# Decoding, splitting and storing a kernel's weights in tiles of 1024 columns instead of 512

## The chip, the cores and the metric

The kernel runs on one core of a Trainium2 chip. The core has TensorE (PE, matrix products), VectorE (DVE), ScalarE (ACT) and GpSimd (POOL) for work on tiles, and SyncE (SP), which here issues all DMAs. Each engine takes its instructions in the order of its own queue. The metric is device time in microseconds (us), the median of several runs; the profile is of one execution.

## What is computed

Causal attention with a decay bias, then two feed-forward layer pairs, all in float32. The inputs are q, k and v of 4 batches, 8 heads, 576 tokens and 64 columns, so 2304 tokens of 512 columns pass the layers:

```python
scores = scale * np.matmul(q, k.transpose(0, 1, 3, 2))
cum = np.cumsum(np.maximum(s, 0.0), axis=-1)
bias = -(cum[:, :, :, None] - cum[:, :, None, :])
scores = np.where(causal, -1000000000.0, scores + np.minimum(bias, 0.0))
attn = softmax(scores)                          # divided by (sum + 1e-09)
x = np.matmul(attn, v)                          # 2304 x 512
x = ((x @ w_a) * (x @ w_b)) @ w_out             # 512 -> 1536 -> 512
h = x @ w_in                                    # 512 -> 2048
out = (np.maximum(h, 0.0) + alpha * np.minimum(h, 0.0)) @ w2_out
```

The weights come as 64-bit floats.

## The kernel before

**Tokens and layers.** The 2304 tokens are taken in five blocks, four of 512 and one of 256 (block 4). `ffn` runs the two layer pairs for a block; the attention of the next block is cut into steps that are laid between its matmuls. A weight tile is 128 x 512; there are 68 (`NW`), and each block uses all of them in the same order, 36 in the first layer pair and 32 in the second. PE multiplies in three parts for precision: a weight tile and its input are each split into a high and a low part (`wh`, `wl`; `xh`, `xl`; `gh`, `gl`), and `mm3` adds high x high, high x low and low x high. So a tile costs PE twelve matmuls.

**The first pair** (`into`, `copy_a`, `gate`): in a step, two tiles make a and b in two PSUM banks, ACT copies a (`a_sb`), DVE multiplies it by b (`g`), and g is split into `gh` (ACT) and `gl` (DVE or POOL). One step later a third tile multiplies it into the output. After the last step there are no tiles for a and b, so the last output tile follows right behind the one before it. **The second pair** (`into`, `rectify`): one tile makes h, ACT, DVE or POOL, and DVE make `m` and `g` from it, g is split, and two steps later another tile multiplies it.

**Weights in block 0.** A raw tile of 64-bit values is loaded (`first`, buffers `raw`, 6), decoded into 32-bit floats by `decode` (one operation on ACT or POOL, then a shift and two combining operations on DVE, lines 970 and 271; buffers `w32`, 4, named `w` in the profile's rows), split into `wh` and `wl` (`parts`, `split`; buffers of `wsp`, 6), and the decoded tile is stored to DRAM (`store`, tensor `w_d`). A `w32` buffer is free again when it has been split and its store has landed (`keep`). **From block 1 on** (`again`, `load_pair`) two decoded tiles come in one load from `w_d` into a raw buffer and are only split. The split of a tile waits for a `wsp` buffer, which PE gives back with the last matmul of a tile (`run.give(of_w)`). `prefetch` starts the loads up to ten tiles (`AHEAD`) ahead of the one that PE takes.

**Other users of the buffers.** From batch 2 on (`STACK`), `stack` splits keys and queries into two `w32` buffers for each head.

**Order.** The code is written out in a fixed order by a planner (`Order`): chains of operations are Python generators, and each `yield` names the engines that may do the next operation with a time in ns. The planner keeps a clock for each engine, takes the operation that could start first, and lets the cheaper engine do it; `slack` (`SL_LOAD`, `SL_PARTS`) puts weight work behind other work of the same time. `Slots` count buffers: a chain that yields one waits until another gives it back. PE's order is that of the loops. A long operation thus changes where the planner puts all others. `sub` goes to POOL or DVE, `copy` to ACT or DVE; those marked `port` are planned as excluding POOL.

## Time and profile before

| | us |
|---|---|
| median of 3 runs (lowest, highest) | 1017.45 (1015.12, 1019.9) |
| profiled execution | 1020.0 |
| its span, first to last instruction | 1018.2 |
| PE busy | 994.2 |
| DVE busy | 730.7 |
| ACT busy | 562.3 |
| POOL busy | 238.4 |

The busy times are sums over the span, in which a record of a pipelined matmul overlaps the next one's. The page further gives slices of the span, the DMA queues, the chain of work that ended last and the costliest groups of instructions; the trace behind it answers for stretches of time, for single lines and tiles, and for who waited for whom. PE's idle time before an instruction is put down to the work that ended the wait.

### The profile page before, as it was taken

What the parts mean: (1) busy time and instruction counts of PE and PEld (TensorE: products, weight loads), DVE (VectorE), ACT (ScalarE), POOL (GpSimd) and SP (SyncE); (2) the same over time, 40 slices, a digit from 0 to 9 for tenths busy, and PEclk for the clock granted to TensorE, in tenths of its full rate; (3) what the DMA queues carried; (4) which work ended last, traced back from release to release, by engine and by line L of the source; (5) the groups of instructions that cost most, each with busy time, mean ns of one, the idle gap of its engine ahead of it and who ended that gap; (6) DMA issues with size and microseconds to landing.
All of it is one profiled execution on the core that took longest, in us unless ns stands there. A gap on an engine that the chain in (4) does not pass through costs nothing.

```text
span 1018.2 us, 16187 instructions
## 1 busy us (share of the span) xinstructions
PE 994.2 (98%) x5385; PEld 813.5 (80%) x5385; DVE 730.7 (72%) x1702; ACT 562.3 (55%) x1166; POOL 238.4 (23%) x300
## 2 busy tenths in 40 slices
PE   6999999999899999999999999999999999999998
PEld 5567777777678888788888888888888888889997
DVE  6998898899887867777468687964454465546685
ACT  5876565676665455655455355654433354446664
POOL 2031111221013233443232123432010022220032
PEclk9999999999999999999999999999999999999999
DMA  7687968466868767657286757464542623417550
GB/s 191 185 263 257 303 222 269 155 234 217 297 229 262 252 182 242 181 171 230 88 264 208 243 191 221 160 188 156 183 141 72 197 69 129 134 48 260 186 182 26
DMA packets 129893, 195.75 MB, mean 192 GB/s; under 512 B 26576, under 2 KB 62416, under 8 KB 129808
## 3 DMA queue, kind: packets, MB, share of 16 engines
q1 hardware_dynamic: 129808, 194.71, 60.6%
q8 instruction: 42, 0.69, 0.3%
q14 instruction: 43, 0.35, 0.1%
HBM read 157.63 MB, written 37.04 MB: 191 GB/s over the span
## 4 chain that ended last, share of the span: by engine, by line
PE 86%; DVE 7%; DMA 5%; ACT 1%; issue 1%; SPq 0%; POOL 0%; ACTq 0%; DVEq 0%; POOLq 0%
PE bank L1060 19%; PE bank L1061 19%; PE bank L1062 19%; PE bank L1169 6%; PE bank L1170 6%; PE bank L1171 6%; DMA w_d<-w 3%; DVE w L271 3%; PE bank L487 2%; DMA kq<-in_kq_a_dram 2%; PE bank L751 2%; PE bank L691 1%; PE bank L513 1%; PE bank L718 1%; PE bank L758 1%
## 5 line engine op out<-in xcount | busy, mean ns | idle before, releaser
L1060 PE MATMUL bank<-xh,wh 128*128 128x512 f32 (+1 forms) x800 | 300.6, 376 | 3.1 <-DVE g L271 2.3
L1062 PE MATMUL bank<-xh,wl 128*128 128x512 f32 (+1 forms) x800 | 295.2, 369 | 1.0 <-DVE wl L277 0.8
L1061 PE MATMUL bank<-xl,wh 128*128 128x512 f32 (+1 forms) x800 | 294.9, 369 | 0.0
L265 ACT ACTIVATE wh<-raw 128x512 fp32r<-128x512 f32 x268 | 167.6, 627 | 99.0 <-PE bank L1061 59.3
L277 DVE TENSOR_TENSOR wl<-raw,wh 128x512 fp32r<-128x512 f32 x188 | 131.4, 700 | 96.5 <-ACT wh L265 89.4
L277 POOL TENSOR_TENSOR wl<-raw,wh 128x512 fp32r<-128x512 f32 x84 | 110.6, 1317 | 340.4 <-ACT wh L265 309.5
L1060 PEld LDWEIGHTS bank<-xh,wh 128*128 128x128 f32 x800 | 150.8, 188 | 34.6 <-issue 5.2
L1062 PEld LDWEIGHTS bank<-xh,wl 128*128 128x128 f32 x800 | 150.8, 188 | 28.2 <-DVE wl L277 2.3
L1061 PEld LDWEIGHTS bank<-xl,wh 128*128 128x128 f32 x800 | 150.9, 189 | 24.3
L265 ACT ACTIVATE gh<-g 128x512 fp32r<-128x512 f32 (+1 forms) x140 | 82.3, 588 | 75.2 <-DVE g L271 73.0
L1169 PE MATMUL bank<-wh,gh 128*128 128x512 f32 x288 | 114.4, 397 | 0.2 <-ACT wh L265 0.2
L1170 PE MATMUL bank<-wl,gh 128*128 128x512 f32 x288 | 112.8, 392 | 1.3 <-DVE wl L277 1.3
L277 DVE TENSOR_TENSOR gl<-g,gh 128x512 fp32r<-128x512 f32 (+1 forms) x125 | 85.5, 684 | 37.6 <-ACT gh L265 36.0
L1171 PE MATMUL bank<-wh,gl 128*128 128x512 f32 x288 | 112.3, 390 | 0.0
L257 ACT ACTIVATE z<-z,mn 128x128 f32<-128x128 f32 (+4 forms) x144 | 83.0, 579 | 41.6 <-DVE mn L271 41.6
L271 DVE SCALAR_TENSOR_TENSOR w<-raw,w 128x512 int32<-128x512 int32 x136 | 92.2, 702 | 0.1
L1060 PE MATMUL bank<-gh,wh 128*128 128x512 f32 (+1 forms) x240 | 90.6, 377 | 1.6 <-ACT gh L265 1.6
L1061 PE MATMUL bank<-gl,wh 128*128 128x512 f32 (+1 forms) x240 | 88.8, 370 | 0.4 <-DVE gl L277 0.4
L1062 PE MATMUL bank<-gh,wl 128*128 128x512 f32 (+1 forms) x240 | 88.5, 369 | 0.0
L257 ACT ACTIVATE m<-bank 128x512 f32<-128x512 f32 (+1 forms) x80 | 44.3, 553 | 69.9 <-PE bank L1062 69.6
L282 DVE TENSOR_SCALAR m<-m,alpha_sb 128x512 f32<-128x512 f32 (+1 forms) x71 | 34.7, 489 | 47.3 <-ACT m L257 46.2
L265 ACT ACTIVATE a_sb<-bank 128x512 f32<-128x512 f32 (+1 forms) x60 | 33.1, 551 | 64.0 <-PE bank L1062 62.0
(96 smaller groups left out, 1422.3 us busy)
## 6 DMA issues: line engine op xcount, KB each, us to landing
raw<-w_d SPq DMA_DIRECT2D x136, 512.0 KB, 4.5
raw<-in_w_dram SPq DMA_DIRECT2D x68, 512.0 KB, 4.8
w_d<-w SPq DMA_DIRECT2D x68, 256.0 KB, 3.5
kq<-in_kq_a_dram SPq DMA_DIRECT2D x16, 512.0 KB, 5.0
zd<-zt SPq DMA_DIRECT2D x32, 192.0 KB, 3.2
pt<-zd SPq DMA_DIRECT2D x32, 192.0 KB, 3.7
kq<-in_kq_b_dram SPq DMA_DIRECT2D x16, 352.0 KB, 7.5
vb<-in_v_dram SPq DMA_DIRECT2D x80, 64.0 KB, 4.0
```

What stands on the lines that cost most here:

```text
L257: nc.scalar.activation(o, i, func, **k)
L265: nc.scalar.activation(o, i, AF.Copy)
L271: f(*args, **k)
L277: (nc.gpsimd if eng == "pool" else nc.vector).tensor_tensor(o, i0, i1, op=ALU.subtract)
L282: (nc.gpsimd if eng == "pool" else nc.vector).tensor_scalar(o, i, s0, s1, op0=ALU.mult, op1=ALU.mult)
L487: nc.tensor.matmul(d, qs[:, r * P:n], k[:, 0:n], start=i == 0, stop=i == 1)
L1060: nc.tensor.matmul(o, wh, ih, start=first, stop=False)
L1061: nc.tensor.matmul(o, wh, il, start=False, stop=False)
L1062: nc.tensor.matmul(o, wl, ih, start=False, stop=last)
L1169: nc.tensor.matmul(acc[t], gh[:, c], wh, start=first, stop=False)
L1170: nc.tensor.matmul(acc[t], gh[:, c], wl, start=False, stop=False)
L1171: nc.tensor.matmul(acc[t], gl[:, c], wh, start=False, stop=last)
```

## The change

Two tiles are now one unit of 128 x 1024 (`W2`; 34 of them, `NP`). In block 0, `first` loads the two raw tiles in two DMAs into one buffer, and `decode`, the split into `wh` and `wl`, and the store each take the whole unit in one instruction. From block 1 on, `load_four` brings four decoded tiles in one DMA of 1 MB; they are split as two units. `take` hands PE one half of a unit at a time, and `leave_w` gives the split buffer back after the second half. All buffers hold as many bytes as before and half as many units: `raw` 3, `w32` 2, `wsp` 3; `AHEAD` is 5 units. `stack` takes one unit for a head's keys and queries. The planner's times follow the size.

```diff
-FROM_WEIGHTS, AHEAD, FROM_LEAD, FROM_STEPS, STEPS = 2, 10, 3, 4, 3
+FROM_WEIGHTS, AHEAD, FROM_LEAD, FROM_STEPS, STEPS = 2, 5, 3, 4, 3
...
-    wsp = ctx.enter_context(tc.tile_pool(name="wsp", bufs=6))
+    wsp = ctx.enter_context(tc.tile_pool(name="wsp", bufs=3))
...
-    W32, RAW, KQ, VB, CB, KL = 4, 6, 3, 4, 3, 2
+    W32, RAW, KQ, VB, CB, KL = 2, 3, 3, 4, 3, 2
...
-        kh = wraw.tile([P, QA], F32R, name="kh", tag="w32", bufs=W32)
-        qs = wraw.tile([P, QA], F32R, name="qs", tag="w32", bufs=W32)
+        hq = wraw.tile([P, 2 * QA], F32R, name="hq", tag="w32", bufs=W32)
+        kh, qs = hq[:, 0:QA], hq[:, QA:2 * QA]
...
+    W2, NP = 2 * WN, NW // 2
...
-        eng = yield {"act": 517, "pool": 590}, SEEN
+        eng = yield {"act": 90 + 0.833 * W2, "pool": 32 + 1.09 * W2}, SEEN
...
-        yield from dve(WN, 0.52, ts, w, w, 3, None, op0=ALU.logical_shift_left,
+        yield from dve(W2, 0.52, ts, w, w, 3, None, op0=ALU.logical_shift_left,
...
-    def load_pair(i):
+    def load_four(i):
         yield of_raw
-        w = wraw.tile([P, 2, WN], F32, name="raw", tag="raw", bufs=RAW)
-        pairs[i, "w"] = w
-        yield from dma(w, w_d[i:i + 2].rearrange("c p n -> p c n"))
+        n = min(4, NW - i)
+        w = wraw.tile([P, 4, WN], F32, name="raw", tag="raw", bufs=RAW)
+        fours[i, "w"] = w
+        yield from dma(w[:, 0:n, :], w_d[i:i + n].rearrange("c p n -> p c n"))
...
         def first():
             yield of_raw
-            r = wraw.tile([P, 2 * WN], I32, name="raw", tag="raw", bufs=RAW)
-            yield from dma(r, w64[i].bitcast(I32))
+            r = wraw.tile([P, 2 * W2], I32, name="raw", tag="raw", bufs=RAW)
+            for j in range(2):
+                yield from dma(r[:, j * W2:(j + 1) * W2], w64[2 * i + j].bitcast(I32))
             yield of_w32
-            w = wraw.tile([P, WN], I32, name="w32", tag="w32", bufs=W32)
+            w = wraw.tile([P, W2], I32, name="w32", tag="w32", bufs=W32)
...
-            h = wsp.tile([P, WN], F32R, name="wh", tag="wh")
-            l = wsp.tile([P, WN], F32R, name="wl", tag="wl")
+            h = wsp.tile([P, W2], F32R, name="wh", tag="wh")
+            l = wsp.tile([P, W2], F32R, name="wl", tag="wl")
...
-            elif i % 2:
+            elif i % 2 or i == NP - 1:
                 run.give(of_raw, run.t)
...
-            yield from dma(w_d[i].bitcast(I32), source[0])
+            yield from dma(
+                w_d[2 * i:2 * i + 2].rearrange("c p n -> p c n").bitcast(I32),
+                source[0].rearrange("p (c n) -> p c n", c=2),
+            )
...
     def prefetch():
-        while len(loaded) < min(taken + ahead, NB * NW):
+        while len(loaded) < min(taken // 2 + ahead, NB * NP):
...
+        return [t[:, n % 2 * WN:(n % 2 + 1) * WN] for t in got]
+
+    def leave_w():
+        nonlocal left
+        left += 1
+        if left % 2 == 0:
+            run.give(of_w)
...
-                    run.give(of_w)
+                    leave_w()
```

PE's instructions keep their number, sizes and order. On the other engines the planner's order moves. Three places, in the order in which the instructions stand in each queue (numbers tell one buffer or tile from another):

DVE, late in block 0, second layer pair. Before: `w32_2786` and `w32_2828` are the decoded tiles 58 and 59 (counted from 0), and `g_2910` is the product of the twelfth step:

```order
L271 SCALAR_TENSOR_TENSOR w32_2786<-raw_2681,w32_2786 128x512
L277 TENSOR_TENSOR wl_2882<-w32_2737,wh_2881 128x512
L271 SCALAR_TENSOR_TENSOR w32_2828<-raw_2703,w32_2828 128x512
L282 TENSOR_SCALAR m_2901<-m_2901,alpha_sb_94 128x512
L271 TENSOR_SCALAR w32_2854<-w32_2854 128x512
L271 SCALAR_TENSOR_TENSOR g_2910<-bank3_98,m_2901 128x512
L271 SCALAR_TENSOR_TENSOR w32_2786<-raw_2681,w32_2786 128x512
L271 SCALAR_TENSOR_TENSOR w32_2828<-raw_2703,w32_2828 128x512
L277 TENSOR_TENSOR gl_2918<-g_2910,gh_2917 128x512
L277 TENSOR_TENSOR wl_2926<-w32_2786,wh_2925 128x512
L277 TENSOR_TENSOR wl_2935<-w32_2828,wh_2934 128x512
```

After: `w32_2454` is the unit of tiles 58 and 59, `w32_2478` the next; `g_2543` and `g_2600` are the products of the eleventh and twelfth step:

```order
L271 TENSOR_SCALAR w32_2454<-w32_2454 128x1024
L271 SCALAR_TENSOR_TENSOR w32_2454<-raw_2367,w32_2454 128x1024
L277 TENSOR_TENSOR gl_2499<-g_2492,gh_2498 128x512
L271 TENSOR_SCALAR w32_2478<-w32_2478 128x1024
L271 SCALAR_TENSOR_TENSOR w32_2454<-raw_2367,w32_2454 128x1024
L282 TENSOR_SCALAR m_2529<-m_2529,alpha_sb_94 128x512
L271 SCALAR_TENSOR_TENSOR w32_2478<-raw_2420,w32_2478 128x1024
L271 SCALAR_TENSOR_TENSOR g_2543<-bank2_97,m_2529 128x512
L277 TENSOR_TENSOR gl_2568<-g_2543,gh_2567 128x512
L282 TENSOR_SCALAR m_2587<-m_2587,alpha_sb_94 128x512
L271 SCALAR_TENSOR_TENSOR w32_2478<-raw_2420,w32_2478 128x1024
L271 SCALAR_TENSOR_TENSOR g_2600<-bank3_98,m_2587 128x512
```

The last decode step of tiles 58 and 59 stood behind the product of the twelfth step and stands ahead of that of the eleventh now.

ACT, block 0, the last steps of the first layer pair. Rows `w32<-raw` are the first operation of a decode. Before, `a_sb_2006` is the last copy of a:

```order
L265 ACTIVATE gh_1949<-g_1937 128x512
L970 ACTIVATE w32_1895<-raw_1821 128x512
L970 ACTIVATE w32_1960<-raw_1839 128x512
L970 ACTIVATE w32_1983<-raw_1872 128x512
L265 ACTIVATE pt2_111<-bank0_95 128x384
L265 ACTIVATE a_sb_2006<-bank2_97 128x512
L265 ACTIVATE wh_1999<-w32_1870 128x512
L265 ACTIVATE pt3_112<-bank1_96 128x384
L265 ACTIVATE wh_2030<-w32_1895 128x512
L970 ACTIVATE w32_2024<-raw_1916 128x512
L265 ACTIVATE gh_2046<-g_2040 128x512
```

After, the same copy is `a_sb_1789`, and the split of the last g is `gh_1823`:

```order
L559 ACTIVATE z_1723<-cb1_1215,cumq_115 128x576
L971 ACTIVATE w32_1717<-raw_1635 128x1024
L265 ACTIVATE gh_1737<-g_1731 128x512
L265 ACTIVATE wh_1773<-w32_1674 128x1024
L265 ACTIVATE pt2_111<-bank0_95 128x384
L265 ACTIVATE a_sb_1789<-bank2_97 128x512
L265 ACTIVATE pt3_112<-bank1_96 128x384
L265 ACTIVATE wh_1807<-w32_1717 128x1024
L265 ACTIVATE gh_1823<-g_1818 128x512
L971 ACTIVATE w32_1801<-raw_1682 128x1024
```

Three decodes stood in a row ahead of the copy, with one operation between; now the nearest stands four rows up, and the next one comes behind the last g's split.

DVE, block 4, where the first layer pair ends. `g_10215` before and `g_9213` after are the last product of the pair, `xl` the low part of the second pair's input:

```order
L277 TENSOR_TENSOR wl_10196<-raw_10098,wh_10195 128x512
L271 TENSOR_TENSOR g_10215<-bank3_98,a_sb_10197 128x256
L277 TENSOR_TENSOR wl_10214<-raw_10098,wh_10213 128x512
L277 TENSOR_TENSOR gl_10224<-g_10215,gh_10223 128x256
L277 TENSOR_TENSOR wl_10238<-raw_10138,wh_10237 128x512
L277 TENSOR_TENSOR xl0_105<-bank4_99,xh0_103 128x256
```

```order
L277 TENSOR_TENSOR wl_9181<-raw_9093,wh_9180 128x1024
L271 TENSOR_TENSOR g_9213<-bank3_98,a_sb_9196 128x256
L277 TENSOR_TENSOR wl_9212<-raw_9093,wh_9211 128x1024
L277 TENSOR_TENSOR gl_9220<-g_9213,gh_9219 128x256
L277 TENSOR_TENSOR xl0_105<-bank4_99,xh0_103 128x256
L277 TENSOR_TENSOR xl0_105<-bank5_100,xh0_103 128x256
```

The product, one low part of a weight and the low part of the product follow each other before and after; the weight's part is 1024 wide now.

## Rows read from the trace of the kernel before

**Rows 1.** The page: busy us, share of the span and instructions of each engine.

```profile
PE 994.2 (98%) x5385; PEld 813.5 (80%) x5385; DVE 730.7 (72%) x1702; ACT 562.3 (55%) x1166; POOL 238.4 (23%) x300
```

**Rows 2.** Busy time by stretch: late in block 0, and block 3; columns as shown.

```profile
core 0: us, PE busy (x) PEld busy (x) DVE busy (x) ACT busy (x) POOL busy (x), PEclk, DMA share, GB/s
...
200.00:290.00 90.00, 86.82 (x436) 64.75 (x435) 82.90 (x166) 59.67 (x115) 14.24 (x20) 1.00 0.74 251
...
720.00:915.00 195.00, 195.00 (x923) 160.29 (x922) 98.62 (x172) 83.03 (x145) 31.24 (x35) 1.00 0.39 126
```

**Rows 3.** Waits of PE, whole run: us in total, times, longest us.

```profile
PE bank L718 <- DVE z L282: 3.1, 2, 2.0
PE bank L1060 <- DVE g L271: 2.3, 1, 2.3
PE bank L513 <- DMA kq<-in_kq_a_dram: 2.1, 2, 1.1
PE bank L1060 <- ACT gh L265: 1.6, 1, 1.6
PE bank L1170 <- DVE wl L277: 1.3, 3, 0.6
PE bank L1062 <- DVE wl L277: 0.8, 2, 0.4
PE bank L1060 <- ACT wh L265: 0.6, 1, 0.6
...
PE bank L1061 <- DVE gl L277: 0.4, 2, 0.2
```

**Rows 4.** Timeline of PE: start us, us, instruction [idle us before <- who ended it].

```profile
48.51 0.66 PE L718 MATMUL bank<-ident,z 128*128 128x128 f32 x4 [1.06 <-DVE z L282]
...
175.71 0.49 PE L1060 MATMUL bank<-gh,wh 128*128 128x512 f32 x1 [1.59 <-ACT gh L265]
...
260.19 0.50 PE L1060 MATMUL bank<-xh,wh 128*128 128x512 f32 x1 [0.59 <-ACT wh L265]
```

**Rows 5.** Waits of ACT from 56 to 290 us.

```profile
ACT w L970 <- DMA w_d<-w: 18.4, 11, 5.2
```

**Rows 6.** Busy time by stretch, with the columns of rows 2: behind the gh wait.

```profile
176.00:184.00 8.00, 7.77 (x49) 4.68 (x49) 5.48 (x12) 4.65 (x10) 1.77 (x2) 0.79 0.86 285
```

**Rows 7.** Timeline of DVE: decode operations, one and two in a row.

```profile
165.91 0.68 DVE L271 SCALAR_TENSOR_TENSOR w<-raw,w 128x512 int32<-128x512 int32 x1
...
167.18 1.28 DVE L271 SCALAR_TENSOR_TENSOR w<-raw,w 128x512 int32<-128x512 int32 x2
```

**Rows 8.** Timeline of ACT: two high parts in a row.

```profile
162.41 1.14 ACT L265 ACTIVATE wh<-w 128x512 fp32r<-128x512 f32 x2
```

**Rows 9.** The page's DMA issues: count, KB each, median us to landing.

```profile
raw<-in_w_dram SPq DMA_DIRECT2D x68, 512.0 KB, 4.8
w_d<-w SPq DMA_DIRECT2D x68, 256.0 KB, 3.5
```

**Rows 10.** Instructions on w_d: issue ns min/median/max, first and last start us.

```profile
L288 SPq DMA_DIRECT2D w_d<-w x68: 319/327/1053, 37.7 to 287.0; - x68
```

**Rows 11.** The chain that ended last: start us, us, what.

```profile
254.99 8.91 DMA w_d<-w
```

**Rows 12.** Timeline of all engines, block 4, where its first layer pair ends.

```profile
964.90 0.63 ACT L265 ACTIVATE wh<-raw 128x512 fp32r<-128x512 f32 x1 [0.42 <-PE bank L1061]
...
965.56 0.69 DVE L277 TENSOR_TENSOR wl<-raw,wh 128x512 fp32r<-128x512 f32 x1
...
966.17 0.42 DVE L277 TENSOR_TENSOR gl<-g,gh 128x256 fp32r<-128x256 f32 x1
...
966.64 0.39 PE L1061 MATMUL bank<-gl,wh 128*128 128x256 f32 x1 [0.17 <-DVE gl L277]
```

**Rows 13.** Timelines of DVE and of POOL ahead of the g wait.

```profile
420.21 0.48 DVE L282 TENSOR_SCALAR m<-m,alpha_sb 128x512 f32<-128x512 f32 x1
...
421.45 1.40 DVE L282 TENSOR_SCALAR m<-m,alpha_sb 128x512 f32<-128x512 f32 x1
...
420.95 3.03 POOL L277 TENSOR_TENSOR wl<-raw,wh 128x512 fp32r<-128x512 f32 x2 [3.71 <-ACT wh L265]
```

More of the change, by code (lines that the diff above doesn't have):

```diff
@@ L236, in attention_two_moe_kernel @@
     of_raw, of_kq, of_w32, of_w, of_vb, of_t, of_pb, of_c0, of_c1, of_kl = (
-        Slots(n) for n in (RAW, KQ, W32, 6, VB, 4, 1, CB, 2, 0)
+        Slots(n) for n in (RAW, KQ, W32, 3, VB, 4, 1, CB, 2, 0)
     )
@@ L492, in q_k @@
                 kq_t.pop((b, hp, 0))
-                for s in (of_kl, of_w32, of_w32, of_stack) * 2:
+                for s in (of_kl, of_w32, of_stack) * 2:
                     run.give(s)
@@ L956, in attention_two_moe_kernel @@
     w_d = dram.tile([NW, P, WN], F32, name="w_d")
-    pairs, turns = {}, {}
+    fours, turns = {}, {}
     loaded = []
-    taken = 0
+    taken = left = 0
     ahead = 0
+    W2, NP = 2 * WN, NW // 2
     def decode(r, w):
@@ L1016, in again @@
             if i % 2 == 0:
-                pairs[i] = run.spawn(load_pair(i))
-            yield pairs[i - i % 2]
-            source.append(pairs[i - i % 2, "w"][:, i % 2, :])
+                fours[i] = run.spawn(load_four(2 * i))
+            yield fours[i - i % 2]
+            w = fours[2 * (i - i % 2), "w"]
+            source.append(w.rearrange("p c n -> p (c n)")[:, i % 2 * W2:(i % 2 + 1) * W2])
         def parts():
             yield turns[n]
-            h = wsp.tile([P, WN], F32R, name="wh", tag="wh")
-            l = wsp.tile([P, WN], F32R, name="wl", tag="wl")
+            h = wsp.tile([P, W2], F32R, name="wh", tag="wh")
+            l = wsp.tile([P, W2], F32R, name="wl", tag="wl")
             got.extend((h, l))
-            yield from split(f32(source[0]) if n < NW else source[0], h, l)
-            if n < NW:
+            yield from split(f32(source[0]) if n < NP else source[0], h, l)
+            if n < NP:
                 run.spawn(keep(stored), run.t)
-            elif i % 2:
+            elif i % 2 or i == NP - 1:
                 run.give(of_raw, run.t)
@@ L1040, in load_w @@
         source = []
-        fetched = run.spawn(first() if n < NW else again(), slack=SL_LOAD)
-        stored = run.spawn(store()) if n < NW else None
+        fetched = run.spawn(first() if n < NP else again(), slack=SL_LOAD)
+        stored = run.spawn(store()) if n < NP else None
         turns[n] = run.spawn(acquire())
@@ L1154, in ffn @@
                     if d == KD - 1:
-                        run.give(of_w)
+                        leave_w()
                     yield
@@ L1175, in ffn @@
                     if t == T // P - 1:
-                        run.give(of_w)
+                        leave_w()
                     yield
```

13 lines of the change are left out of this document (6 added, 7 removed).

## The prediction, made before the changed kernel ran

> **What bounds the kernel now.** I read the busy shares first, then the stages, then what TensorE (PE) waited for, then those waits in their place. PE is busy for 98% of the span [rows 1]: 1018.2 - 994.2 = 24.0 us idle in all. From block 1 on there is nearly nothing to win: in block 3 PE is busy for all of 195.00 us, 923 matmuls, 211 ns each [rows 2]. In the last 90 us of block 0 VectorE (DVE) is busy for 92% of the time, and that is the only long stretch where another engine comes near PE [rows 2]. So the change, which cuts no matmul, can only take away or add PE waits, and their list is the whole budget [rows 3]. The longest of the z waits (2.0) and the longer kq wait (1.1) fall in the opening, before any weight is decoded. What is left: 1.1 for z, 1.0 for kq, 2.3 for g, 1.6 and 0.4 for gh and gl, and 1.3 + 0.8 + 0.6 = 2.7 for weights; together 9.1 us. The first of the weight waits that I show is at 260.19 us [rows 4]; all lie in that last stretch of block 0, where a tile's split ends just as PE wants it. Behind the gh wait at 175.71 us the granted clock fell to 0.79 over 8 us [rows 6], between the two levels of 1.2 and 2.4 GHz, worth 0.21 x 8 = 1.7 us more. Ceiling: about 10.8 us, 1.1%.
>
> What feeds PE in block 0: a raw tile lands, ScalarE (ACT) and three DVE operations decode it, ACT and DVE or GpSimd (POOL) split it, and it is stored. The decoded buffer is free again when split and store are done, and the ACT queue stands still if its next decode finds none: 18.4 us in eleven waits on stores, the longest 5.2 us [rows 5].
>
> **The change part by part.** PE's own rows are the same in number, size and order, so nothing is added there.
>
> *Twice the size, half the count.* One decode step of 512 columns takes 0.68 us, two in a row 1.28 [rows 7]; so a second one in the row costs 0.60. One operation of 1024 columns I cost between 1.1 (0.60 + 0.60, less a fixed part) and 1.28; two 512-wide splits on ACT take 1.14 [rows 8], so a double one between 1.0 and 1.14. On DVE the decode goes from 204 operations to 102. The fixed part of each is at most 0.68 - 0.60 = 0.08 us by these rows, so 102 x 0.08 = 8 us at most of DVE time, and at least none. It lies beside PE and is worth nothing by itself; what counts is which product comes when in DVE's row.
>
> *Block 0, weights late in the row.* The order shows it: before, the last decode steps of tiles 58 and 59 stand behind the g of the twelfth step of the second layer pair's loop; now those of their pair stand ahead of the g of the eleventh. That is one step, two tiles, 24 matmuls x 211 ns = 5.1 us earlier against PE's own course. A pair must be split whole before its first tile is used, which gives back one more half split: 1.28 - 0.68 = 0.6 on DVE, or some 1.5 if the split is on POOL, where two took 3.03 [rows 13]. Left over: 3 to 4 us, more than the longest of these waits, 0.6 [rows 3]. I take all **2.7 us** off; the ends are 2.7 gained and 2.7 lost again (same waits, doubled).
>
> *The opening.* The decode steps of the first tiles stood between the z's of the last heads; one pair is now decoded there where four tiles were begun. The z wait at 48.51 us, 1.06 [rows 4], goes: **1.1 us**, at least none. The kq wait I leave, since that load stands behind two raw loads now, not one; the row gives 1.0 either way.
>
> *The wait at 175.71 us.* Before, three decodes stand in one row on ACT right ahead of the a_sb of the last gate step; the third waits 5.2 us for a store [rows 5], a_sb is late, g, gh after it, and PE stands for 1.59 us [rows 4]. Now the decode next ahead of that a_sb is four rows up, and the next one comes after gh. With the 0.2 for gl and the 1.7 of the clock 3.5 us hang on it. A larger store may hold that one decode for longer, so I take two thirds, **2.3 us**; ends none and 3.5.
>
> *Block 4, a loss.* There a tile takes half as long. At the change from the first layer pair to the second, DVE's row is g, wl, gl before and after, but the wl between is 1024 wide and so is the wh that ACT does ahead of gh. By [rows 12] wh starts at 964.90 for 0.63, wl at 965.56, gl at 966.17 for 0.42, and PE already waits 0.17. Doubled, wh takes 1.0 to 1.14 and ends near 966.0, wl holds DVE's row for 1.1 to 1.28 until 967.1, gl ends at 967.5; PE's matmul moves from 966.64 to 967.55, so **0.9 us** lost. In blocks 0 to 3 the tile of the last gate step's output lasts 12 x 211 ns = 2.5 us, which covers the same extra 0.9; where that cover is gone it is 0.9 a block.
>
> *Stores of 512 KB and two buffers.* Storing 256 KB takes 3.5 us to land, loading 512 KB 4.8 [rows 9]; I take 4.8 for the new store, with 3.5 and the longest of the chain, 8.91 [rows 11], as ends. Each wait on ACT may be 1.3 longer, but ACT has 32 decodes in the new order, not 66, so the sum of them stays near 18 us, in other places. Behind a waiting decode stand a_sb, gh and wh. ACT is idle for a third of that stretch [rows 2], so most of it is covered; I add **1.5 us** for new PE waits (one like the 1.59), ends none and 9, the price of the slower rival on stores below.
>
> *Loads by four from block 1 on.* The same bytes in half as many loads. PE never waits there for a raw tile (no such row in [rows 3]), and three buffers of four hold the twelve tiles that six of two held. Nothing; if one were late it would be a few us once.
>
> Sum: -2.7 - 1.1 - 2.3 + 0.9 + 1.5 = -3.7. The profiled execution took 1020.0 us, 2.55 over the median of the runs, 1017.45; so 1020.0 - 3.7 = 1016.3 there, and **1013.8 us** as a median, 0.4% faster.
>
> **The rivals.** *All of it goes* (every wait of the budget, and no new ones but block 4's): 1020.0 - 10.8 + 0.9 - 2.55 = 1007.5. For it: DVE's row is shorter, and each g in it stands earlier. Against it: the g wait of 2.3 lies in block 2, where nothing says that the order gets better.
>
> *Nothing moves*: what the order gives, the pair takes back, because its first tile waits for its second. 1017, plus or minus 2. For it: 3 to 4 us of lead is little beside one store of 8.91.
>
> *Two decoded buffers are too few* (slower). A buffer's round is the ACT decode (1.1), the DVE work from a pair's first to its last decode row (5.2 on average over ten pairs late in block 0, counted in the new order with the durations of [rows 7]), and the store's landing. Two buffers must feed a pair every 2 x (287.0 - 37.7) / 68 = 7.3 us [rows 10], so a round may last 14.7 us, and stores decide it from 14.7 - 6.3 = 8.4 us of landing on. At 8.91 it is 15.2, 0.5 for each of 17 rounds, 9 us, with the gains gone: 1017.45 + 9 = 1026. Against it: the median of 4.8 leaves 3.5 us to spare.
>
> *GpSimd holds DVE up* (slower). A DVE operation on m took 1.40 us, three times the 0.48 of its like, while POOL split a wl [rows 13], and this lies just ahead of the 2.3 us wait for g. The new order has 45 such POOL splits for 104, each twice as long, so one may hold DVE for 1.8 instead of 0.9. PE feels it only at the short margins, the changes between layer pairs, one a block: five at 2 us, -3.7 + 10 = +6.3, hence 1023.8. The Trainium skill (SBUF — State Buffer, section "SBUF: two separate sides") says that GpSimd and VectorE share one pair of ports as an exclusive lock, held for the whole instruction, and that a VectorE operation with two SBUF inputs needs it too. By that rule every wl on POOL would block the split and decode steps of DVE for its whole length, which is this rival. The trace agrees for the one operation above; how often it happens at 1024 columns no run shows yet.
>
> **How the numbers follow.** The forecast (1010.5 to 1016.5) has 0.38, all goes 0.24, nothing moves 0.17, too few buffers 0.11, the port 0.10. A measurement of this kernel tells about 0.5%, 5.1 us: below 1012.4 is faster, above 1022.5 slower. Faster: 0.23 of the second case and a third of the forecast, 0.13: 0.36. Slower: most of the last two and a little of the third: 0.20. The same: 0.44. The range goes from 1006.5, where the best case ends, to 1027, past the two slower ones; about 0.15 stays outside.
>
> **What would show it.** In the new profile: no PE wait on wl or wh between 225 and 285 us; no wait for z near 48; the clock at 1.00 from 176 to 184; a PE wait for gl near 1 us in block 4's change. Wrong would be: PE waits on wh behind ACT decodes that wait on stores landing after more than 8.4 us (two buffers), or DVE operations of 2 us beside POOL's wl and PE waits for g behind them (port).

## The result and the profile after

The changed kernel takes 1028.12 us (median of six runs, 1027.45 to 1029.61), the kernel before 1016.5 beside it (six runs, 1014.73 to 1019.9): a ratio of 1.0109, with a 95% interval of 1.009 to 1.0128 (an estimate over the runs; the two medians divide to 1.0114). It is slower by 1.1%; forecast were 1013.8 us and a range up to 1027.0. The profiled execution of the changed kernel took 1028.74 us with a span of 1026.9, that of before 1020.0 with 1018.2; so 8.7 us of the 11.6 can be followed in the two traces (the profiled execution of before lies 3.5 us over its median, that of the changed kernel 0.6).

The page's busy line, which answers [rows 1], and the stretches, which answer [rows 2] (columns as there):

```profile
PE 994.4 (97%) x5385; PEld 813.9 (79%) x5385; DVE 728.0 (71%) x1475; ACT 540.6 (53%) x977; POOL 211.8 (21%) x240
```

```profile
200.00:290.00 90.00, 82.72 (x419) 63.10 (x420) 75.17 (x111) 53.21 (x86) 15.24 (x16) 0.96 0.72 241
290.00:510.00 220.00, 214.74 (x1134) 177.51 (x1133) 158.92 (x344) 113.08 (x213) 69.04 (x76) 0.98 0.64 201
720.00:915.00 195.00, 195.00 (x923) 160.04 (x922) 102.88 (x154) 78.20 (x111) 13.03 (x19) 1.00 0.38 126
```

PE does the same work in as many instructions; block 3 is still full. PE idles for 7.3 of the 90 us late in block 0 (3.2 before), and for 5.3 us between 290 and 510 (2.3 before), both with a clock below 1.00. The waits of PE after the opening, which answer [rows 3]:

```profile
PE bank L1074 <- ACT wh L265: 5.1, 1, 5.1
PE bank L1074 <- DVE g L271: 4.0, 2, 3.5
PE bank L1075 <- DVE gl L277: 2.0, 2, 1.1
PE bank L1185 <- DVE gl L277: 1.9, 3, 0.8
PE bank L1074 <- DVE sm L271: 1.5, 1, 1.5
PE bank L1076 <- POOL wl L277: 1.4, 1, 1.4
PE bank L1074 <- ACT a_sb L265: 1.3, 1, 1.3
```

Two of these are long, wh and g. To see what each place is worth, I took from the timelines of PE the start of the first matmul of the same weight tile (0 to 67 are block 0, 272 to 339 block 4):

| tile | before, us | after minus before |
|---|---|---|
| 0 | 56.2 | -4.0 |
| 34 | 171.2 | -4.5 |
| 36 | 183.8 | -8.5 |
| 47 | 221.8 | -3.0 |
| 50 | 231.4 | -3.8 |
| 62 | 275.6 | -7.3 |
| 64 | 285.3 | -2.7 |
| 68 (block 1) | 296.2 | +0.4 |
| 100 | 395.6 | +0.4 |
| 136 (block 2) | 510.9 | +5.4 |
| 272 (block 4) | 915.8 | +6.0 |
| 339 | 1011.9 | +9.8 |
| end of span | 1018.2 | +8.7 |

The changed kernel was 7.3 us ahead at tile 62. It lost 7.7 us by tile 68, 5.0 in the second half of block 1 and 3.8 in block 4 up to its last tile; 1.1 comes back behind it. These are the three places that the experiments take up. There is a fourth: between tiles 36 and 47 the lead falls from 8.5 to 3.0 us, behind waits for sm (the softmax sums, 1.46 us at 185.31), gl (0.83), VectorE's wl (0.39) and POOL's wl (1.36 at 214.73), where the kernel before has no wait. No run isolates it.

**The end of block 0.** What ACT and PE did there:

```profile
275.26 1.13 ACT L971 ACTIVATE w<-raw 128x1024 f32<-128x1024 f32 x1 [2.96 <-DMA raw<-in_w_dram]
...
281.51 1.06 ACT L265 ACTIVATE wh<-w 128x1024 fp32r<-128x1024 f32 x1 [1.64 <-DVE w L271]
```

```profile
282.62 0.80 PE L1074 MATMUL bank<-xh,wh 128*128 128x512 f32 x1 [5.09 <-ACT wh L265]
```

PE's wait names wh, but read backwards it is a raw tile: ACT could not begin the decode of tiles 64 and 65 before 275.26, because the raw load had not landed; from there decode, DVE's steps and wh take the usual time. SP's queue says why. First the longest wait of SP from 262 to 268 us, then SP's row, then the landing of the two raw loads of that stretch (count, KB each, median us from issue):

```profile
SPq L288 <- DVE w L271: 3.0, 1, 3.0
```

```profile
259.43 0.35 SPq L288 DMA_DIRECT2D raw<-in_w_dram  x1
...
266.41 0.38 SPq L288 DMA_DIRECT2D raw<-w_d  x1
266.83 0.50 SPq L288 DMA_DIRECT2D w_d<-w  x1
267.39 1.23 SPq L288 DMA_DIRECT2D raw<-in_w_dram  x2
```

```profile
raw<-in_w_dram SPq DMA_DIRECT2D x2, 512.0 KB, 8.2
```

A unit's raw load is two transfers of 512 KB, and the code orders the second by itself, after the first has landed by the planner's reckoning. So the second halves of the last two units stand behind block 1's first load by four. That load needs a buffer of 1 MB, which VectorE's last decode step of the unit before gives back at 266.35; then its 1 MB goes first, and the two halves come in at 275 and 276.5 (8.2 us from issue, where all such loads of the run have a median of 5.7). Behind the wait the clock falls; PE busy, granted clock, DMA share and GB/s:

```profile
280.00:288.00 8.00, 5.34 (x15) 0.60 0.63 188
...
424.00:432.00 8.00, 4.49 (x11) 0.65 0.44 140
```

The mean of 0.60 in the first lies near the lower of the two levels of 1.2 and 2.4 GHz. 0.40 x 8 = 3.2 us is a bound on what it costs, since PE stood idle until 282.62 of those 8 us; by the starts of tiles 64 and 66, between which PE waits for nothing, it cost 2.1 us.

**Block 1.** The second row above lies behind the wait for g. DVE, POOL and PE there, to be read beside [rows 13]:

```profile
423.02 2.71 DVE L282 TENSOR_SCALAR m<-m,alpha_sb 128x512 f32<-128x512 f32 x1
```

```profile
423.07 2.37 POOL L277 TENSOR_TENSOR wl<-raw,wh 128x1024 fp32r<-128x1024 f32 x1 [4.28 <-ACT wh L265]
```

```profile
427.57 0.80 PE L1074 MATMUL bank<-xh,wh 128*128 128x512 f32 x1 [3.51 <-DVE g L271]
```

The operation on m, 0.48 us as a rule, lasts for 2.71, until 0.3 us after GpSimd's split has ended at 425.44. Before, it was 1.40 beside a split of half the width. The wait for g grows from 2.3 to 3.5, and the clock now falls (0.35 x 8 + 0.07 x 8 = 3.4 us as a bound; tiles 108 to 110, behind the wait, lose 2.6). The change between the layer pairs adds 1.07 us for gl at 406.35, and there too GpSimd's split stands beside it; DVE and POOL:

```profile
403.87 2.42 DVE L277 TENSOR_TENSOR gl<-g,gh 128x512 fp32r<-128x512 f32 x1
```

```profile
403.35 2.39 POOL L277 TENSOR_TENSOR wl<-raw,wh 128x1024 fp32r<-128x1024 f32 x1 [0.42 <-ACT wh L265]
```

gl takes 0.69 us as a rule.

**Block 4.** ACT and PE near the start, then all engines at the change between the layer pairs, which answers [rows 12]:

```profile
924.74 1.06 ACT L265 ACTIVATE wh<-raw 128x1024 fp32r<-128x1024 f32 x1 [1.21 <-PE bank L1075]
925.70 0.36 ACT L265 ACTIVATE a_sb<-bank 128x256 f32<-128x256 f32 x1
```

```profile
926.12 0.39 PE L1074 MATMUL bank<-xh,wh 128*128 128x256 f32 x1 [1.30 <-ACT a_sb L265]
```

```profile
972.44 1.06 ACT L265 ACTIVATE wh<-raw 128x1024 fp32r<-128x1024 f32 x1 [0.93 <-PE bank L1075]
...
973.53 1.23 DVE L277 TENSOR_TENSOR wl<-raw,wh 128x1024 fp32r<-128x1024 f32 x1 [0.54 <-ACT wh L265]
...
974.67 0.42 DVE L277 TENSOR_TENSOR gl<-g,gh 128x256 fp32r<-128x256 f32 x1
...
975.15 0.39 PE L1075 MATMUL bank<-gl,wh 128*128 128x256 f32 x1 [0.91 <-DVE gl L277]
```

The second is what the prediction described, 0.91 us. The first it did not: wh, twice as long and free to start only when PE gives back a whole pair of buffers, stands ahead of a_sb. With 0.53 for g and 0.38 for gl a little later it makes 3.1 us.

### The profile page after: what moved, and what is told of

The parts are those of the page before. It is cut to its first block, busy times and chain, and to the rows that moved or that the text cites. A ratio compares the mean times of both kernels' runs of the same rounds, so it can differ in the third digit from the quotient of the medians.

```text
span 1026.9 us, 15259 instructions
## 1 busy us (share of the span) xinstructions
PE 994.4 (97%) x5385; PEld 813.9 (79%) x5385; DVE 728.0 (71%) x1475; ACT 540.6 (53%) x977; POOL 211.8 (21%) x240
## 4 chain that ended last, share of the span: by engine, by line
PE 84%; DVE 7%; DMA 4%; issue 2%; ACT 2%; SPq 0%; POOL 0%; ACTq 0%; POOLq 0%; DVEq 0%
PE bank L1074 20%; PE bank L1075 19%; PE bank L1076 19%; PE bank L1183 5%; PE bank L1185 5%; PE bank L1184 5%; DVE w L271 2%; PE bank L486 2%; PE bank L750 2%; DMA w_d<-w 1%; PE bank L512 1%; PE bank L717 1%; PE bank L690 1%; PE bank L757 1%; DVE z L271 1%
## 5 line engine op out<-in xcount | busy, mean ns | idle before, releaser
L265 ACT ACTIVATE wh<-raw 128x1024 fp32r<-128x1024 f32 x134 | 141.6, 1057 | 72.8 <-PE bank L1075 50.4
L277 DVE TENSOR_TENSOR wl<-raw,wh 128x1024 fp32r<-128x1024 f32 x99 | 121.2, 1224 | 79.8 <-ACT wh L265 79.4
L277 POOL TENSOR_TENSOR wl<-raw,wh 128x1024 fp32r<-128x1024 f32 x37 | 90.1, 2434 | 259.8 <-ACT wh L265 168.0
L277 DVE TENSOR_TENSOR gl<-g,gh 128x512 fp32r<-128x512 f32 (+1 forms) x125 | 99.8, 800 | 35.0 <-ACT gh L265 34.7
L271 DVE SCALAR_TENSOR_TENSOR w<-raw,w 128x1024 int32<-128x1024 int32 x68 | 82.9, 1228 | 0.3
L271 DVE TENSOR_TENSOR g<-bank,a_sb 128x512 f32<-128x512 f32 (+1 forms) x60 | 38.1, 634 | 46.5 <-PE bank L1076 43.2
```

Source lines behind the costliest of these rows:

```text
L265: nc.scalar.activation(o, i, AF.Copy)
L271: f(*args, **k)
L277: (nc.gpsimd if eng == "pool" else nc.vector).tensor_tensor(o, i0, i1, op=ALU.subtract)
```

## The experiments

Theory: three separate costs, namely (A) the second raw halves behind the first load by four, (B) GpSimd's wider splits that hold VectorE, (C) splits and buffers in twos at the short margins. The rivals are named run by run. Ratios are to the kernel before in the same set, with 95% intervals. The kernel before had medians of 1016.5, 1017.6, 1017.0 and 1018.1 us in the four sets, so medians of two sets are compared to a us or two. The profiled execution can lie some us off the median; the last three columns are of it alone: what it lost against the kernel before from the start of one tile to that of another (50 to 68: late in block 0; 100 to 136: second half of block 1; 272 to 339: block 4).

| run | median, us | ratio | profiled, us | 50 to 68 | 100 to 136 | 272 to 339 |
|---|---|---|---|---|---|---|
| the changed kernel | 1028.12 | 1.0109 (1.0090 to 1.0128) | 1028.74 | 4.2 | 5.0 | 3.8 |
| e1_halves_last | 1021.13 | 1.0047 (1.0024 to 1.0070) | 1026.20 | -0.6 | 5.3 | 3.8 |
| e2_pool_halves | 1025.22 | 1.0085 (1.0057 to 1.0113) | 1024.47 | 4.2 | -0.9 | 3.8 |
| e4_halves_both | 1019.66 | 1.0030 (1.0003 to 1.0057) | 1021.89 | 0.0 | 1.9 | 3.8 |
| e9_four_later | 1021.60 | 1.0039 (1.0016 to 1.0063) | 1020.80 | 1.4 | 0.2 | 3.8 |
| e5_loads_two | 1025.82 | 1.0087 (1.0061 to 1.0112) | 1022.29 | 4.4 | 0.2 | 2.3 |
| e3_split_single | 1015.27 | 0.9988 (0.9967 to 1.0010) | 1017.19 | -5.0 | 1.6 | 1.1 |
| e6_shared_buffers | 1025.80 | 1.0075 (1.0051 to 1.0100) | 1024.85 | 0.9 | 0.2 | 2.6 |
| e10_wide_no_pool | 1019.17 | 1.0022 (1.0005 to 1.0038) | 1020.97 | -1.0 | -1.2 | 3.8 |
| e7_single_no_pool | 1014.46 | 0.9971 (0.9951 to 0.9991) | 1013.22 | -4.6 | -2.5 | 1.1 |
| e8_before_no_pool | 1013.56 | 0.9970 (0.9951 to 0.9988) | 1014.17 | 0.5 | -2.5 | 0.0 |
| e11_decode_halves | 1025.74 | 1.0068 (1.0047 to 1.0089) | 1021.07 | 2.7 | -2.5 | 1.1 |

**e1_halves_last.**

```diff
-            for j in range(2):
-                yield from dma(r[:, j * W2:(j + 1) * W2], w64[2 * i + j].bitcast(I32))
+            if n < NP - 2:
+                for j in range(2):
+                    yield from dma(r[:, j * W2:(j + 1) * W2], w64[2 * i + j].bitcast(I32))
+            else:
+                yield {"sp": 960}, 700
+                for j in range(2):
+                    nc.sync.dma_start(r[:, j * W2:(j + 1) * W2], w64[2 * i + j].bitcast(I32))
+                yield {"dma": 2 * P * W2 / 90}, 900
```

> The raw load of a unit of two tiles is two transfers, each put into SP's queue by itself. In the changed kernel the second halves of the last two units of block 0 stand behind the first load by four, for which SP waits 2.90 us, and TensorE then waits 5.09 us for wh at 282.6 us. Here the two halves of these two units alone are issued back to back, ahead of that load. Theory A (the queue is the cause): the 5.09 us wait is gone, and the granted clock of 0.60 from 280 to 288 us is 1.00 again, worth 0.40 x 8 = 3.2 us: 1028.1 - 8.3 = 1019.8 us. Rival (VectorE's decode or the two decoded buffers make wh late, whatever the load does): the wait stays above 4 us and the time at 1028.

1021.13 us, 7.0 less. From 250 to 290 us PE waits 0.7 for pt and 0.5 for wl and no longer for wh, and the clock is back:

```profile
280.00:288.00 8.00, 7.95 (x35) 1.00 0.67 210
```

Cause A holds: late in block 0 the order of SP is worth 4.8 us (4.2 lost in the changed kernel, -0.6 here). The median gained more, and the profiled execution only 2.5 us, which began with 2.0 us less lead at tile 0 and still has block 1's wait for g (3.50) with the lower clock. It took 1026.2 us and one other 1025.9; the remaining six of the eight took 1018.1 to 1021.5, less by about what that wait and its clock cost. They may have been without it, but they left no trace. So of the 7.0 us part may belong to B.

**e9_four_later.** Another way: the halves stay apart, the load by four goes behind them.

```diff
...
     def load_four(i):
+        yield brought[NP - 1]
         yield of_raw
...
-        def first():
+        def bring():
             yield of_raw
             r = wraw.tile([P, 2 * W2], I32, name="raw", tag="raw", bufs=RAW)
+            raws[n] = r
             for j in range(2):
                 yield from dma(r[:, j * W2:(j + 1) * W2], w64[2 * i + j].bitcast(I32))
+
+        def first():
+            brought[n] = run.spawn(bring(), run.t, slack=SL_LOAD)
+            yield brought[n]
+            r = raws[n]
```

> The changed kernel, but the first load by four may be queued only behind the last raw load of block 0; the two halves of a unit's raw load stay apart. In SP's row only that one load moves, behind the two raw halves that stood behind it; the store ahead of them, which waits for the same decode until 266.4 us, stays. It tells the 1 MB that went ahead of them from SP's standing still. If the bytes of the load by four are what made the raw halves late (they landed 7.8 and 8.6 us after issue): issued near 266.9 us, landed by 272.5 instead of 275.2 and 276.5, the 5.09 us wait for wh below 2.5: about 1023 us, as in the kernel with loads by two. If the 2.90 us for which SP stood still is the whole cause: the wait stays above 4 us and the time near 1027. If both halves' place counts, as e1 has it, only the edit of e1 reaches 1021.

1021.60 us. SP's row and, from 262 to 272 us, the landing of the two halves (count, KB each, median us from issue):

```profile
266.11 0.38 SPq L288 DMA_DIRECT2D w_d<-w  x1
266.53 1.34 SPq L288 DMA_DIRECT2D raw<-in_w_dram  x2
...
269.92 0.54 SPq L288 DMA_DIRECT2D raw<-w_d  x1
```

```profile
raw<-in_w_dram SPq DMA_DIRECT2D x2, 512.0 KB, 4.8
```

SP stands still as long as before (3.0 us, until 266.11), now for the store ahead of the halves. What changed is what goes in front of them: 4.8 us to land in place of 8.2, and ACT's decode starts at 270.98 in place of 275.26. The wait for wh is gone; one of 2.62 for POOL's wl takes its place, half as long, and with no fall of the clock. That wait comes from the new order: the planner now gave this unit's low part to GpSimd, where VectorE had done it in 1.22 us:

```profile
277.07 3.21 POOL L277 TENSOR_TENSOR wl<-w,wh 128x1024 fp32r<-128x1024 f32 x1 [7.98 <-ACT wh L265]
```

So the 1 MB ahead of the halves made them late by 3.4 us. Late in block 0 that is worth 2.8 of the 4.8 us of e1; what is left may be GpSimd's low part or SP's standing still, which this run does not tell apart. The rest of its gain lies in block 1, where m is not held (see e4): the profiled execution has 0.2 us there for 5.0. Eight of its ten executions took 1020.4 to 1022.8 us, two 1027.9 and 1028.0.

**e5_loads_two.**

```diff
-        yield from dma(w[:, 0:n, :], w_d[i:i + n].rearrange("c p n -> p c n"))
+        for j in range(0, n, 2):
+            yield from dma(w[:, j:j + 2, :], w_d[i + j:i + j + 2].rearrange("c p n -> p c n"))
```

> The changed kernel, but from block 1 on each load of four tiles is cut into two of two tiles each, the second queued by itself behind the first, into the same buffers. The prediction costed the load by four at nothing; it may also be what SP holds the raw loads back for at the end of block 0. If the load by four costs nothing: 1027 to 1029. If its size is what keeps the last raw loads of block 0 or the first weights of block 1 late: the wait for wh at 282.6 us (5.09) shrinks and the time is 1020 to 1024.

1025.82 us, between the two expectations, and by the intervals no different from the changed kernel. With 512 KB ahead of them the halves take 6.1 us to land, between 8.2 and 4.8; PE waits 2.17 for wh, then 2.11 for POOL's wl (GpSimd has this unit's low part here too) and 1.39 for gl. Late in block 0 it loses 4.4 us, as much as the changed kernel: the shorter landing gained nothing in the end. That its profiled execution is 6.4 us below that of the changed kernel is cause B (m is not held in this trace, the wait for g is 1.28) and block 4, where a_sb stands ahead of the second wh in ACT's row and PE does not wait for it.

**e2_pool_halves.**

```diff
+        if eng == "pool" and n == 1024:
+            for j in range(2):
+                c = slice(j * 512, (j + 1) * 512)
+                nc.gpsimd.tensor_tensor(o[:, c], i0[:, c], i1[:, c], op=ALU.subtract)
+            return
         (nc.gpsimd if eng == "pool" else nc.vector).tensor_tensor(o, i0, i1, op=ALU.subtract)
```

> Every split of 1024 columns that the order gives to GpSimd is issued as two of 512, one right behind the other; no other row of any engine moves. Theory B (GpSimd holds VectorE for the length of one of its instructions): the operation on m that took 2.71 us at 423.0 us, beside a split of 2.37, takes at most 1.6; the wait for g at 427.6 falls from 3.51 to about 2.3, as in the kernel before, and the clock of 0.65 and 0.93 from 424 to 440 us (2.8 + 0.6 us) is back at 1.00: 1028.1 - 1.2 - 3.4 = 1023.5 us. Rival (the whole GpSimd work counts, however it is cut, or m was late for another reason): the wait stays at 3.5 and the time at 1028.

1025.22 us, 2.9 less where 4.6 were expected; the intervals overlap. The place did as forecast and more; DVE and POOL:

```profile
423.58 0.49 DVE L287 TENSOR_SCALAR m<-m,alpha_sb 128x512 f32<-128x512 f32 x1
```

```profile
423.63 2.83 POOL L280 TENSOR_TENSOR wl<-raw,wh 128x512 fp32r<-128x512 f32 x2 [4.26 <-ACT wh L265]
```

m is not held at all, the wait for g is 1.29 and the clock from 424 to 440 us is 1.00. Of the 3.5, then, 2.2 are GpSimd's, as long as m was held (2.71 - 0.49); 1.3 would be there without it. But m went free in e9 and e5 as well, beside a split of full width, so this does not yet show that the cut did it. What shows the length is gl, which is held here too, for one short split instead of a long one, and the wait for it is gone:

```profile
405.49 1.33 DVE L282 TENSOR_TENSOR gl<-g,gh 128x512 fp32r<-128x512 f32 x1
```

**e4_halves_both**, the two edits together.

> The edits of the first two kernels of this set together. If the loss is made of these two places, the gains add: 1028.1 - 8.3 - 4.6 = 1015.2 us, the kernel before or a little below it. If one wait only moves to the other place, or TensorE was covered at one of them, less than 8 us is gained: above 1020.

1019.66 us, 8.5 less than the changed kernel, but 4.5 more than expected, since here m is held again (1.62 us at 418.25, POOL's pair of splits starting at 418.30), g is waited for 2.42 us, and the clock falls to 0.95 and 0.84 from 416 to 432 us. Against e1, whose m was held for 2.70 us beside a split of 2.37, the hold is as much shorter as the single instruction on GpSimd is (1.29), and the wait for g with it (3.50 to 2.42). In e9 the order at this place is that of the changed kernel, and m is not held:

```profile
419.90 0.49 DVE L282 TENSOR_SCALAR m<-m,alpha_sb 128x512 f32<-128x512 f32 x1
```

```profile
419.95 2.66 POOL L277 TENSOR_TENSOR wl<-raw,wh 128x1024 fp32r<-128x1024 f32 x1 [4.27 <-ACT wh L265]
```

The two records start 0.05 us apart with DVE first, here and in e1, e2, e5, e9 and the changed kernel alike: DVE gets through in e2, e5 and e9, and is held in the other three (in e1 for 2.70). In e9 GpSimd's split is the longer one instead, 2.66 for 2.37. Which of the two goes first hangs on less than the records tell apart, and the changed kernel had the bad end of it in the execution profiled; all its six lie between 1027.45 and 1029.61 us.

**e10_wide_no_pool.** The edit of e1, and the low parts from block 1 on not on GpSimd:

```diff
...
-        eng = yield Either(pool=115 + 2.17 * n, dve2=t) if sbuf else {"dve": t}, SEEN
+        can = Either(pool=115 + 2.17 * n, dve2=t) if pool else {"dve2": t}
+        eng = yield can if sbuf else {"dve": t}, SEEN
...
-            yield from split(f32(source[0]) if n < NP else source[0], h, l)
+            yield from split(f32(source[0]) if n < NP else source[0], h, l, pool=n < NP)
```

> The edit of e1_halves_last, and the low parts of the weights' splits of blocks 1 to 4 on VectorE alone; the splits stay 1024 wide and the buffers are given back by twos. e1 took 1021.1 us and its profile has a wait for g of 3.50 us with a clock of 0.57 over 8 us (3.4). Theory B (GpSimd's split is the cause of that wait): both go, 1021.1 - 6.9 = 1014.2 us; what is then left against e7 (1014.5) is the width itself, 2.7 us in block 4, so 1014 to 1017. Rival (the wide split holds VectorE's row just as long when VectorE does it itself): a wait for g or gl of more than 2 us stays between 400 and 430 us, and the time is 1019 or more.

1019.17 us, between the two. All that PE waits for from 290 us on:

```profile
PE bank L1081 <- DVE g L271: 1.8, 2, 1.3
PE bank L1081 <- ACT a_sb L265: 1.3, 1, 1.3
PE bank L1082 <- DVE gl L278: 0.9, 1, 0.9
PE bank L1192 <- DVE gl L278: 0.7, 2, 0.4
```

The wait for g is down to 1.28 with the clock at 1.00, and that for gl near 406 us is gone with the splits still 1024 wide, so B holds, for both waits of block 1; I had counted the whole 3.5 as gained. The sum also began at e1's median, which lies 5.1 us under its profiled execution, 1026.2, the one that showed the wait and the lower clock; so part of that was not in the median to be won. The waits of block 4 are what they were (3.8 us lost): C is apart from B. (In this profile the clock was also at 0.60 from 64 to 72 us, 3.2 us that belong to none of the three.)

**e3_split_single.** Decode, store and loads stay as changed; the split is by single tiles.

```diff
-    wsp = ctx.enter_context(tc.tile_pool(name="wsp", bufs=3))
+    wsp = ctx.enter_context(tc.tile_pool(name="wsp", bufs=6))
...
-        def parts():
-            yield turns[n]
-            h = wsp.tile([P, W2], F32R, name="wh", tag="wh")
-            l = wsp.tile([P, W2], F32R, name="wl", tag="wl")
+        def parts(m, got):
+            yield turns[m]
+            h = wsp.tile([P, WN], F32R, name="wh", tag="wh")
+            l = wsp.tile([P, WN], F32R, name="wl", tag="wl")
             got.extend((h, l))
-            yield from split(f32(source[0]) if n < NP else source[0], h, l)
+            s = source[0][:, m % 2 * WN:(m % 2 + 1) * WN]
+            yield from split(f32(s) if n < NP else s, h, l)
...
```

> Decode and store by units of two and the loads by four stay; the split alone is undone: 512 columns each into six buffers, each tile given back by itself. Theory C (the wider split is late at the changes between layer pairs and in block 4, where ScalarE's wh of 1.06 us stands ahead of a_sb and gh): the waits for a_sb (1.30) and gl and g (0.91, 0.53, 0.38) of block 4 and that for gl at 406.4 us (1.07) go, 4.2 us, and with GpSimd's splits at 512 the 1.2 + 3.4 us around 427 us as well; the wait for wh at 282.6 us stays, since the raw loads are queued as before: 1028.1 - 8.8 = 1019.3 us. Rival (the width of the split is not what costs, only its place in the order): 1027 to 1029.

1015.27 us, 12.9 less: the whole loss. The main waits of PE (ovl is the low part of the attention's output that a later block takes):

```profile
PE bank L690 <- DVE ovl L277: 3.4, 2, 3.1
PE bank L1078 <- DVE g L271: 2.3, 1, 2.3
...
PE bank L1078 <- ACT a_sb L265: 0.9, 1, 0.9
```

In block 4 1.1 us are lost for 3.8, with a_sb at 0.88 and the rest gone; gl at 406 is gone, g is back at 2.3, with GpSimd's splits at 512. But the wait for wh went too, which I had not expected: the planner's order moved with the splits, and only one of the two late raw halves still stands behind the load by four. This run therefore undoes A as well, and its time does not say what C alone is worth. Block 4 does: the runs on A and B (e1, e2, e4, e9 and e10) all lose 3.8 us there, so the 2.7 us that e3 wins back there are C's, with what its new order moved.

**e6_shared_buffers**: two splits of 512 into halves of one buffer, which comes back only as a whole.

```diff
...
+            c = slice(m % 2 * WN, (m % 2 + 1) * WN)
+            if m % 2 == 0:
+                both.append(wsp.tile([P, W2], F32R, name="wh", tag="wh"))
+                both.append(wsp.tile([P, W2], F32R, name="wl", tag="wl"))
+            h, l = both[0][:, c], both[1][:, c]
...
```

> As e3_split_single, 512 columns in each split instruction, but the two halves of a unit are written into one double buffer, three in all, which is given back only when both tiles are used, as in the changed kernel. It tells the length of one instruction from the return of buffers by twos. Theory C1 (the length of one instruction on ScalarE, VectorE and GpSimd is what costs): the waits are as in e3, 1015 to 1017 us. Rival C2 (the buffers that come back by twos make both halves late): the waits for a_sb (1.30) and gl (0.91) in block 4 and for gl near 406 us (1.07) stay, about 3.3 us: 1018.5 us or more.

1025.80 us. Of the waits of PE from 56 us on:

```profile
PE bank L690 <- DVE ovl L277: 5.0, 2, 3.1
...
PE bank L1086 <- ACT a_sb L265: 1.4, 1, 1.4
```

For block 4 it answers in two parts. gl at the change between the layer pairs is down from 0.91 to 0.17: there it was the length of the instruction (C1). (gl at 406 us is gone as well, but that is GpSimd's, as e10 has it.) PE still waits 1.39 for a_sb, which speaks for the buffers that come back by twos (C2); but e5 has no such wait with the same buffers, and e3 has 0.88 without them. In these runs PE waits for a_sb where a_sb stands behind a wh that waits for a buffer of PE's, and the planner's order decides that. Most of what this run lost against e3 lies in block 0, where the split units are late again (PE waits 2.48 for wh at 275.5) and the clock fell three times to 0.79; how much of that is the buffers and how much the new order I could not separate.

**e7_single_no_pool and e8_before_no_pool**: e3, and the kernel before, each without GpSimd's weight splits from block 1 on (the edit shown at e10).

> e3_split_single, with the low parts of the weights' splits of blocks 1 to 4 on VectorE alone, never on GpSimd; in e3 TensorE waits 2.32 us for g at 420 us, where an operation on m is held beside GpSimd's split, and the clock is at 0.82 and 0.96 from 416 to 432 us (1.4 + 0.3 us). Theory B: the wait and the lower clock go: 1015.3 - 4.0 = 1011.3 us. Rival (VectorE, with more of its own to do, is late elsewhere): 1015 or more, with waits for g, gl or wl in blocks 1 to 3.

> The kernel before, with the low parts of the weights' splits of blocks 1 to 4 on VectorE alone. It shows what GpSimd costs without the change, and what is left for the change when that is gone. Theory B: the 2.3 us wait for g at 424 us goes, with no clock to win back there: 1017.6 - 2.3 = 1015.3 us. Rival (VectorE is late elsewhere): 1017 or more.

1014.46 us, between its two expectations, and 1013.56, below its own: faster than the kernel before by 0.3% each, and the only two whose intervals say so. Waits of PE from 56 us on, two of e7 and the longest of e8:

```profile
PE bank L691 <- DVE ovl L278: 4.7, 2, 3.1
...
PE bank L1079 <- ACT a_sb L265: 0.9, 1, 0.9
```

```profile
PE bank L1061 <- ACT gh L265: 1.4, 1, 1.4
```

The wait for g near 420 us is gone in both. Between them stands what remains of the change (decode and store by two, loads by four): 0.9 us in the medians, nothing that these intervals can tell. In e7 the weights of block 0 are no longer late, as the prediction had it, but ovl is, for 4.7 us.

**e11_decode_halves**: e7, with VectorE's decode at 512 again.

```diff
...
-        yield from dve(W2, 0.52, ts, w, w, 3, None, op0=ALU.logical_shift_left,
-                       port=True)
...
+        for j in range(2):
+            c = slice(j * WN, (j + 1) * WN)
+            u, hi, lo = w[:, c], high[:, c], low[:, c]
+            yield from dve(WN, 0.52, ts, u, u, 3, None, op0=ALU.logical_shift_left,
+                           port=True)
...
```

> e7_single_no_pool, with the three decode steps on VectorE cut into 512 columns again (ScalarE's first step and the stores stay at 1024). In e7 TensorE waits 3.08 us at 186.1 us and 1.58 at 123.3 for ovl, which stands in VectorE's row behind two decode steps of 1.21 us each. Theory (the length of one decode instruction delays what stands behind it): these two fall by half, 1014.5 - 2.3 = 1012.2 us. Rival (ovl is late because the whole unit stands ahead of it): both waits stay, 1014 to 1016, plus what 102 more fixed parts cost.

1025.74 us, 11 worse, against both expectations. The profiled execution is the shortest of its eight, 4.7 us under the median. In it ovl is no longer waited for, as the theory had it, but the weights are:

```profile
PE bank L1080 <- ACT wh L265: 6.4, 3, 3.0
PE bank L1082 <- DVE wl L278: 4.5, 5, 2.6
```

A unit can be split only when its last step is through. With six short steps in VectorE's row where three long ones stood, there are more places for other work to come between. That is how I read it; no run isolates it.

## Why the prediction was wrong

- **What bounds the kernel**: right. PE's work is unchanged, and its waits and clock are the whole difference. The ceiling of 10.8 us was a bound on gains; it said nothing of what new waits may cost.
- **Sizes**: right. A decode step of 1024 took 1.22 us (1.1 to 1.28 forecast), wh 1.06 (1.0 to 1.14).
- **Weights late in block 0, 2.7 us**: right in its mechanism; the lead grows by 3.5 us from tile 50 to 62, and there is no wait for wh or wl from 225 to 282 us (two of 0.4 and 1.4 stand earlier, at 199 and 215). The sign that was named, none up to 285, failed with the 5.09 us at 282.62.
- **The opening, 1.1 us**: right and under-sized. The z wait near 48 us is gone. Tile 0 comes 4.0 us earlier here and 1.7 to 2.5 in three runs with the same opening (e1, e2 and e4); in those and in the kernel before the clock fell to 0.79 to 0.86 from 16 to 24 us, and in this profile it did not, so near 2 us of the 4.0 are luck.
- **The wait at 175.71 us, 2.3 us**: right as far as it goes. It is gone, with the clock at 1.00 from 176 to 184 us, and the lead grows by 4.0 us from tile 34 to 36. By tile 47 5.5 us were lost again, more than that, with the new waits from 185 to 215 us, for which the sum has no term.
- **Stores and two decoded buffers, a loss of 1.5 us**: not borne out. The store took 3.5 us to land (4.8 taken), and ACT's waits on stores fell from 18.4 us in eleven [rows 5] to 7.6 in four (the row stands below this list). That rival is out.
- **Loads by four, nothing**: this is the step that failed most. The sentence "PE never waits there for a raw tile" was read from the kernel before, whose raw tile is one transfer. In the new code a unit takes two, ordered apart, and the new order of SP, which could be read before the run, has the load by four ahead of two raw halves. I costed the load where it is used, in block 1, and not where it is issued, in block 0. From tile 62 to 68 it is 7.7 us: 5.09 of wait, where the kernel before had 0.5, 2.1 of clock, and 0.7 for gl at 294.20. e1, whose edit is to this order, wins 4.8 us from tile 50 to 68.
- **GpSimd**: the mechanism of the rival with 0.10 was right. Its sizes were 2.2 us for g and 1.07 for gl (2 forecast), its count two places, both in block 1, not five. The forecast itself put the holds at nothing: the wait for g grew by 1.2 us and brought 2.6 of clock that no term had, and with gl block 1 lost 5.0 us.
- **Blocks 1 to 4**: 0.9 at block 4's change was right: PE waits 0.91 for gl where 0.17 stood before, and 1.0 us is lost there. Two more waits close behind it (0.53 and 0.38) were not in the sum. That the cover in blocks 1 to 3 takes up the wider split held: the one wait there, 1.07 us in block 1, is GpSimd's. a_sb (1.30) in block 4 was not seen: I had followed g and gh behind the wider wh, not the copy out of the accumulator that stands behind a wh waiting for its buffer.
- **The range**: its top was one slower rival at a time. Three separate mechanisms came together, 7.7 + 5.0 + 3.8 = 16.5 us of loss against a lead of 7.3 at tile 62, a lead that had already lost 5.5 between tiles 36 and 47.

The waits of ACT on stores from 56 to 290 us in the changed kernel, which answer [rows 5]:

```profile
ACT w L971 <- DMA w_d<-w: 7.6, 4, 3.7
```

## What to carry to other kernels

When two steps are merged, look at what the merged thing needs before it can start and at what it holds until it ends: here two transfers in place of one, a buffer of twice the size, one instruction of twice the length. Cost a moved transfer in the queue where it is issued, beside what stands behind it there, and not only where its data are used. Where a helper engine can hold the main one, the length of its single instruction is what counts, and a short margin should not depend on which of the two comes first. When one execution is profiled and many are timed, compare the same stretch in the traces before you credit an edit with the difference of two medians.

## What the runs showed of the hardware

- A hold between GpSimd and VectorE that is all or nothing. Beside GpSimd's splits an operation on g that reads PSUM kept its 0.69 us, and the transposes kept their 0.57 to 0.85; of the others that read SBUF alone, those on m, gl, kl and z (times its sum) took up to 2.7 in the changed kernel, m 2.71 for 0.49 and gl 2.42 for 0.69. The Trainium skill (SBUF — State Buffer, section "SBUF: two separate sides") says that whichever starts first gets the shared pair of ports for its whole instruction; the lengths agree (m 2.71 beside 2.37 in the changed kernel, GpSimd's wl 2.66 for 2.37 in e9, where m went first). By the records VectorE started 0.05 us ahead in the changed kernel and was held all the same, so the recorded start does not tell who gets the ports.
- The same wait does not always cost the same clock. Behind a wait for g of 2.3 us near 420 us the clock stayed at 1.00 in the kernel before and fell to 0.82 and 0.96 in e3_split_single.
- The landing of two loads of 512 KB went from 4.8 us (e9) to 6.1 (e5) and 8.2 (the changed kernel) with nothing, 512 KB and 1 MB of another load just ahead of them; a store of 512 KB stood ahead of them in all three.
